# Attention and token/channel mixer on one core: q and k turned by VectorE in 32x32 blocks, scores of four heads as four 32-row TensorE tiles

## The chip, the cores and the metric

The kernel runs on one core of a Trainium2 chip. The metric is the device time of one launch in microseconds (us). Three runs of the kernel before gave 339.78, 341.17 and 840.59 us; their median is 341.17 us. The profile is one further execution of the same program.

## What is computed

Eight batches; q, k and v have 8 heads of 576 tokens and 64 features. Attention has a causal mask and a bias that comes from a running sum; behind it stand a mixer over the tokens and one over the channels, each with a residual.

```python
scores = np.matmul(q, k.transpose(0, 1, 3, 2)) / np.sqrt(D)
cum = np.cumsum(np.maximum(s, 0.0), axis=-1)
bias = -(cum[:, :, :, None] - cum[:, :, None, :])
scores = np.where(causal, -1e9, scores + np.minimum(bias, 0.0))
attn = softmax(scores)                       # over the keys
x = matmul(attn, v), heads side by side      # (8, 576, 512)
h = np.maximum(x.T @ w_tok1, 0.0) @ w_tok2   # 576 -> 256 -> 576
u = x + h.T
out = u + np.maximum(u @ w_ch1, 0.0) @ w_ch2 # 512 -> 1536 -> 512
```

## The kernel before, in words

**Layout and loops.** The program handles one batch after another, and in a batch one pair of heads after another (`pair`, L606). The bias is folded into v: v of each head is multiplied by the exponential of the running sum, with an added column of those weights, so that the division at the end gives the softmax. Of the score matrix only the diagonal 128x128 blocks and the ones beside them are computed (five key blocks, `PIECES`, L526); a flag that is worked out on the way sends inputs for which that isn't enough to `general`, which these inputs don't reach.

**The way of q and k** (the part that is changed). `stage_qk` (L563) loads k and q of two heads: 96 partitions, each with six tokens in a row of both heads (288 KB for each DMA, L568). A cast to bf16 on GpSimd (L575; in batch 0 VectorE and ScalarE may take it too) writes `qkn`. In `pair`, TensorE transposes it against the identity, six transposes of 96 columns for k and six for q (L619), into PSUM tiles of the ring `psc`. Copies then put the columns into token order in SBUF: one for k into `kT` (L629 on ScalarE or L631 on VectorE), two for q into `qT` (L639 or L641). `qT` has two planes, one for each head, whose other 64 partitions are zero, so that one matmul over 128 partitions gives one head's scores of 64 features.

**Scores.** Four PSUM tiles a pair, with five matmuls (L657): three of 512 columns, one of 384, one of 128, for both heads together. ScalarE takes the exponential (L663) into `E`, VectorE multiplies the diagonal blocks by the triangle `keep` (L671). Then nine matmuls of 65 columns a head give attention times v (L689) into the ring `pav`; VectorE takes the reciprocal (L698) and writes `x` (L703).

**Mixers.** `tok` (L773): L791 and L812 with the residual add L819, then transposes of u on TensorE (L831) with a copy (L839 or L841). `chan` (L845): L859, 48 matmuls a batch of 512 columns for even and 2x320 for odd batches, with the relu on ScalarE (L866) or VectorE (L868); L877, twelve matmuls for each output tile, the add L888 and the store. These use the ring `pmx`.

**What sets the order.** All of this is recorded as operations with planned durations (`Plan`, L47). `Plan.run` (L95) places them on the engines by readiness and priority, and the program is written out in that order; each engine then takes its instructions strictly in it. A ring (`Ring`, L15) is a set of buffers; `slot_time` (L113) says when the next one is free. PSUM has eight tiles of 512 floats: 3 `psc`, 2 `pav`, 3 `pmx`. In the first 45 planned microseconds gaps on TensorE are filled with matmuls on zeros (L964). The sum of squares of k and q (L588, and L600 with a second load for batches 0 and 1, `stage_sq`) belongs to the flag.

The rings that the change touches, as they stand:

```python
r_qf = ring("qkf", 3, [PR, 2, 2, R, D], FP32)
r_qn = ring("qkn", 3, [PR, 2, R, 2, D], BF16)
r_qT = ring("qT", 3, [128, 2, S], BF16)
r_kT = ring("kT", 3, [128, 640], BF16)
r_E = ring("E", 3, [128, 2, EW], BF16)
```

Of the kernel before, what the change touches and what calls it, by code (L numbers as in the profile page):

```python
# [46 lines left out]
class Plan:  # L47
# [47 lines left out]
    def run(self, eps=0.03):  # L95
# [17 lines left out]
        def slot_time(o):  # L113
            t = 0.0
            want = {}
            for b in o.bufs:
                if b.slot is None:
                    r = b.ring
                    if b.ordered and r.queue[0] is not b:
                        return None  # L120
                    fr = [r.free[i] for i in range(len(r.tiles)) if not r.busy[i]]
                    if not fr:
                        return None
                    t = max(t, min(fr))
                    want[id(r)] = want.get(id(r), 0) + 1
# [208 lines left out]
def kernel(  # L334
# [27 lines left out]
    R = 6  # L362
    PR = S // R

# [65 lines left out]
    def pads(eng, i):  # L430
        eng.memset(r_qT.tiles[i][64:128, 0, :], 0.0)
        eng.memset(r_qT.tiles[i][0:64, 1, :], 0.0)
        eng.memset(r_kT.tiles[i][:, S:640], 0.0)
# [8 lines left out]
    def pads3(eng, p):  # L442
        eng.memset(r_vp[p].tiles[0][64 * (1 - p) : 64 * (1 - p) + 64, NJ - 1, :, :], 0.0)
# [3 lines left out]
    for i in range(1, 3):  # L447
# [13 lines left out]
    wT = sb("wT", [128, NJ + 1, B * H], FP32, fast)  # L461
# [24 lines left out]
    def w_tr():  # L486
        for jc in range(NJ + 1):
            j0 = jc * 128 if jc < NJ else S - 128
            nc.tensor.transpose(out=bw.t[:, jc * 64 : jc * 64 + 64], in_=wn[:, j0 : j0 + 128],
                                identity=identf[:, :])  # L490
    P.op({"PE": (0.7, 1.1, w_tr)}, reads=["wn"], writes=[(bw, 0)], prio=(0,))
    P.op(dve(384, lambda: nc.vector.tensor_copy(
        out=wT[:, :, :].rearrange("p c e -> p (c e)"), in_=bw.t[:, 0:384])),
# [6 lines left out]
    NSQ = B * H // 2  # L500
    sq = sb("sq", [PR, NSQ], FP32, fast)
    junk = sb("junk", [PR, 4 * R * D], BF16, fast)
    pre = sb("pre", [64, S], FP32, fast)
# [22 lines left out]
    PIECES = [[(0, 0, 256)], [(1, 128, 384)], [(2, 256, 512)], [(3, 384, 576), (4, 512, 576)]]  # L526
# [3 lines left out]
    def stage_v(b):  # L530
        vf, vp = Buf(r_vf), Buf(r_vp[b % 2])
        odd = b % 2
        vbuf[b] = vp
        for c in range(NJ):
            n = min(128, S - c * 128)
            p0 = 64 if odd and n < 128 else 0

            def load(c=c, n=n, p0=p0):
                nc.sync.dma_start(out=vf.t[p0 : p0 + n, c, :, :],
                                  in_=v[b, :, c * 128 : c * 128 + n, :].rearrange("h p d -> p h d"))  # L540
            load_op(load, [(vf, c)] + ([("st", "v")] if b == 1 else []), 1024 * 0.0226 / 16 * n / 128)
        for c in range(NJ):
            n = min(128, S - c * 128)
            p0 = 64 if odd and n < 128 else 0

            def mul(eng, c=c, n=n, p0=p0):
                cw = c + 1 if p0 else c
                eng.tensor_tensor(  # L548
                    out=vp.t[p0 : p0 + n, c, :, 0:D], in0=vf.t[p0 : p0 + n, c, :, :],
                    in1=wT[p0 : p0 + n, cw, b * H : b * H + H].unsqueeze(2).to_broadcast([n, H, D]), op=ALU.mult)  # L550
# [4 lines left out]
        def ones():  # L555
            nc.gpsimd.tensor_copy(out=vp.t[:, 0 : NJ - 1, :, D], in_=wT[:, 0 : NJ - 1, b * H : b * H + H])
            p0, cw = (64, NJ) if odd else (0, NJ - 1)
            nc.gpsimd.tensor_copy(out=vp.t[p0 : p0 + 64, NJ - 1, :, D], in_=wT[p0 : p0 + 64, cw, b * H : b * H + H])
        P.op({"POOL": (0.5, 0.7, ones)}, reads=["wT"], writes=[(vp, "w")], prio=b * 10 + 5)

    qkn = {}

    def stage_qk(b, h):  # L563
        f, n = Buf(r_qf), Buf(r_qn)
        qkn[(b, h)] = n
        for i, src in enumerate((k, q)):
            def load(i=i, src=src):
                nc.sync.dma_start(out=f.t[:, i, :, :, :].rearrange("p e r d -> p e (r d)"),  # L568
                                  in_=src[b, h : h + 2, :, :].rearrange("e (p r) d -> p e (r d)", r=R))
# [443 lines left out]
```

## Time and profile before

| what | value |
|---|---|
| three runs | 339.78, 341.17, 840.59 us; median 341.17 |
| span of the profiled execution, first to last instruction | 337.3 us |
| its own device time | the page gives the span alone; the two lower runs lie 2.5 and 3.9 us above it |
| TensorE busy | 315.2 us (93%), granted clock 0.994 |
| ScalarE, VectorE, GpSimd busy | 221.6, 207.7, 100.1 us (66, 62, 30%) |
| DMA | 50.6 MB, 56.7% of 16 engines' time |

Read the table with two things in mind. "Busy" is a union of spans: a matmul's span runs from its first to its last column through the array, so matmuls overlap and a stream of them shows no gap; what one more matmul costs is the distance of starts, not its span. And the share is a mean over stages: in the first 50 us TensorE also runs the zero matmuls, which are there to fill gaps.

### The profile page before, as it was taken

The page shows a single profiled execution, that of the slowest core. Times are in us where ns is not written, and L with a number is a line of the kernel's source. Part 1 is how long each engine was busy: PE and PEld are TensorE (multiplying, and loading weights), DVE is VectorE, ACT ScalarE, POOL GpSimd, SP SyncE. Part 2 cuts the span into 40 slices and gives each one's busy share as a digit, 9 for nine tenths or more (in the row PEclk, how much of TensorE's full clock was granted, in tenths as well). Part 3 has the DMA queues.
Part 4 walks back from the last instruction along what each step waited for, and adds up shares of the span by engine and source line. Part 5 has one row for each costly group of instructions (what it writes and reads, how often), then busy time and mean ns, then how long its engine had stood idle before and what let it go on. Part 6 is the DMA issues. An engine that isn't in the chain of part 4 may idle for free.

```text
span 337.3 us, 6710 instructions
## 1 busy us (share of the span) xinstructions
PE 315.2 (93%) x2532; PEld 184.7 (55%) x2565; DVE 207.7 (62%) x510; ACT 221.6 (66%) x395; POOL 100.1 (30%) x137
## 2 busy tenths in 40 slices
PE   6978999988999999989999999989999999999992
PEld 2445585645765455555765445555765454446641
DVE  7698945899776746584577655584677545450021
ACT  4766975669788548785786747787799738325600
POOL 6355157768237001830147001830110000000000
PEclk9799999999999999999999999999999999999999
DMA  7999999999953349288024952253548110011031
GB/s 203 222 291 376 374 213 231 266 271 227 215 114 106 130 138 206 77 208 194 2 75 133 227 145 71 87 157 121 143 119 232 67 63 2 16 49 62 3 95 68
DMA packets 62584, 50.60 MB, mean 150 GB/s; under 512 B 39632, under 2 KB 55568, under 8 KB 62544
## 3 DMA queue, kind: packets, MB, share of 16 engines
q1 hardware_dynamic: 62544, 50.10, 56.7%
q8 instruction: 22, 0.36, 0.4%
q14 instruction: 18, 0.15, 0.2%
HBM read 40.65 MB, written 9.44 MB: 148 GB/s over the span
## 4 chain that ended last, share of the span: by engine, by line
PE 69%; DVE 18%; ACT 7%; issue 2%; DMA 1%; POOL 1%; SPq 0%; ACTq 0%
PE pmx_118 L877 9%; PE pmx_119 L877 8%; PE pmx_117 L859 8%; PE pmx_118 L859 8%; PE pmx_119 L859 8%; PE pmx_117 L877 7%; DVE ub_101 L819 3%; PE pmx_119 L791 2%; DVE E_86 L671 2%; PE psc_114 L657 2%; PE pav_115 L689 2%; PE psc_113 L657 2%; DVE E_84 L671 2%; PE pav_116 L689 2%; PE psc_112 L657 2%
## 5 line engine op out<-in xcount | busy, mean ns | idle before, releaser
L859 PEld LDWEIGHTS <-wc_70 128*128 128x128 bf16 x624 | 59.3, 98 | 30.5 <-issue 0.2
L877 PEld LDWEIGHTS <-gb_107 128*128 128x128 bf16 x240 | 22.9, 98 | 25.3
L575 POOL CAST qkn_76<-qkf_73 96x768 bf16<-96x768 f32 x22 | 19.1, 887 | 37.5 <-ACT gb_107 L866 20.1
L877 PEld LDWEIGHTS <-ga_106 128*128 128x128 bf16 x192 | 18.2, 98 | 21.2 <-issue 1.4
L575 POOL CAST qkn_77<-qkf_74 96x768 bf16<-96x768 f32 x19 | 15.7, 840 | 40.8 <-ACT ga_106 L866 19.7
L575 POOL CAST qkn_75<-qkf_72 96x768 bf16<-96x768 f32 x19 | 15.4, 828 | 39.1 <-ACT gb_107 L866 18.5
L671 DVE TENSOR_TENSOR E_84<-E_84,keep 128x256 bf16<-128x256 bf16 (+1 forms) x55 | 18.4, 365 | 13.3 <-ACT E_84 L663 12.8
L859 PE MATMUL pmx_118<-uTb_105,wc_70 128*128 128x320 bf16 x128 | 22.6, 299 | 0.1
L859 PE MATMUL pmx_117<-uTb_105,wc_70 128*128 128x320 bf16 x128 | 22.6, 299 | 0.0
L859 PE MATMUL pmx_119<-uTb_105,wc_70 128*128 128x320 bf16 x128 | 22.6, 299 | 0.0
L877 PE MATMUL pmx_119<-wc_71,gb_107 128*128 128x512 bf16 x92 | 22.3, 379 | 0.2
L548 POOL TENSOR_TENSOR vp_90<-vf_88,wT 128x512 bf16<-128x512 f32 (+1 forms) x20 | 21.0, 1069 | 2.5 <-DMA vf_88<-in_v_dram 2.2
L671 DVE TENSOR_TENSOR E_86<-E_86,keep 128x256 bf16<-128x256 bf16 (+1 forms) x50 | 17.1, 368 | 6.7 <-ACT E_86 L663 6.4
L671 DVE TENSOR_TENSOR E_85<-E_85,keep 128x256 bf16<-128x256 bf16 (+1 forms) x55 | 16.5, 329 | 6.3 <-ACT E_85 L663 6.1
L877 PE MATMUL pmx_118<-wc_71,gb_107 128*128 128x512 bf16 x80 | 19.2, 379 | 0.2
L866 ACT ACTIVATE gb_107<-pmx_119 128x320 bf16<-128x320 f32 x25 | 11.1, 444 | 11.4 <-PE pmx_119 L859 9.9
L859 PE MATMUL pmx_118<-uTa_104,wc_70 128*128 128x512 bf16 (+1 forms) x77 | 17.0, 335 | 0.2
L859 PE MATMUL pmx_119<-uTa_104,wc_70 128*128 128x512 bf16 (+1 forms) x79 | 17.1, 336 | 0.1
L548 POOL TENSOR_TENSOR vp_89<-vf_87,wT 128x512 bf16<-128x512 f32 (+1 forms) x15 | 15.3, 1040 | 5.8 <-PE pav_116 L689 4.7
L859 PE MATMUL pmx_117<-uTa_104,wc_70 128*128 128x512 bf16 (+1 forms) x78 | 16.8, 335 | 0.1
L877 PE MATMUL pmx_117<-wc_71,ga_106 128*128 128x512 bf16 x69 | 16.7, 379 | 0.2
L877 PE MATMUL pmx_118<-wc_71,ga_106 128*128 128x512 bf16 x69 | 16.5, 379 | 0.3 <-ACT uTb_105 L839 0.2
(297 smaller groups left out, 723.0 us busy)
## 6 DMA issues: line engine op xcount, KB each, us to landing
qkf_74<-in_k_dram SPq DMA_DIRECT2D x15, 288.0 KB, 3.4
qkf_74<-in_q_dram SPq DMA_DIRECT2D x15, 288.0 KB, 4.0
vf_87<-in_v_dram SPq DMA_DIRECT2D x16, 256.0 KB, 7.0
vf_88<-in_v_dram SPq DMA_DIRECT2D x16, 256.0 KB, 5.5
qkf_72<-in_k_dram SPq DMA_DIRECT2D x13, 288.0 KB, 4.0
qkf_72<-in_q_dram SPq DMA_DIRECT2D x13, 288.0 KB, 4.5
qkf_73<-in_k_dram SPq DMA_DIRECT2D x12, 288.0 KB, 4.7
qkf_73<-in_q_dram SPq DMA_DIRECT2D x12, 288.0 KB, 5.0
```

What stands on the lines that cost most here:

```text
L548: eng.tensor_tensor(out=vp.t[p0 : p0 + n, c, :, 0:D], in0=vf.t[p0 : p0 + n, c, :, :], in1=wT[p0 : p0 + n, cw, b * H : b * H + H].unsqueeze ...
L575: nc.gpsimd.tensor_copy(out=o, in_=a)
L657: nc.tensor.matmul(out=o[:, :, c0 : c0 + e - a], lhsT=kT.t[:, j0 : j0 + 128], rhs=qT.t[:, :, a:e], start=True, stop=True)
L671: nc.vector.tensor_tensor(out=E.t[:, :, d0 : d0 + n], in0=E.t[:, :, d0 : d0 + n], in1=keep[:, k0 : k0 + n].unsqueeze(1).to_broadcast([128, ...
L689: nc.tensor.matmul(out=o[:, ic, 0 : D + 1], lhsT=E.t[:, hh, d0 : d0 + 128], rhs=vp.t[:, jc, h + hh, 0 : D + 1], start=(jc == j_lo), stop=( ...
L791: nc.tensor.matmul(out=pm.t[:, ha * D : hb * D], lhsT=w1[:, NJ if odd and c == NJ - 1 else c, t * 128 : t * 128 + 128], rhs=x.t[:, c, ha * ...
L819: nc.vector.tensor_tensor(out=dst.t[lo:hi, di, :], in0=pm.t[lo:hi, :], in1=x.t[lo:hi, c, :], op=ALU.add)
L859: nc.tensor.matmul(out=pm.t[:, 0 : e - a], lhsT=wc1[:, m, cc * 128 : cc * 128 + 128], rhs=uT.t[:, m, a:e], start=(m == 0), stop=(m == NMC ...
L866: lambda cc=cc, pm=pm, a=a, e=e: nc.scalar.activation(out=g.t[:, cc, a:e], in_=pm.t[:, 0 : e - a], func=AF.Relu),
L877: nc.tensor.matmul(out=pm.t[:, :], lhsT=g.t[:, cc, c * 128 : c * 128 + 128], rhs=wc2[:, cc, :], start=(cc == 0), stop=(cc == NCC - 1))
```

## The change

The counts of heads and buffers change, and with them the way of k and q:

- A load takes one of k or q for four heads: partition 32e+t holds 18 tokens in a row of head e (`[128, 1152]`, 4608 bytes in a row, 576 KB a DMA). Four such buffers.
- VectorE transposes that buffer in 32x32 blocks, in fp32, one instruction for each load (L574 of the changed kernel, STREAM_TRANSPOSE). The features of head e then lie on partitions 32e to 32e+31, in two halves of 32 features.
- GpSimd casts each half to bf16 and puts it in token order (L582; two for k, two for q of four heads; in batch 0 VectorE and ScalarE may take them). TensorE's transposes L619 and the copies L629, L631, L639, L641 are gone, and so are the zeros in `qT`.
- Scores of four heads are computed in two phases. In each, a key block takes two matmuls a head (one for each half of the features, added up in PSUM), each over 32 partitions, with `tile_position` at row 32e and a PSUM tile of its own for each head. That is 40 matmuls for four heads.
- The exponential is taken for one head at a time, 512 columns as before; the mask multiply covers four heads at once.
- PSUM: 4 `psc`, which one phase fills, and 4 `pmx`, which now also take attention times v. `kT`, `qT` and `E` have two buffers, each for four heads.
- The squares read the fp32 load, one instruction for k and one for q of four heads.
- v's last rows lie on the same partitions for even and odd batches. `slot_time` now counts how many buffers of a ring an operation wants. A branch that would transpose u by DMA is added for batches from 9 on (`UDMA = 9`); there are eight, so it is never taken.

Its core as a diff:

```diff
-                    fr = [r.free[i] for i in range(len(r.tiles)) if not r.busy[i]]
-                    if not fr:
+                    fr = sorted(r.free[i] for i in range(len(r.tiles)) if not r.busy[i])
+                    n = want[id(r)] = want.get(id(r), 0) + 1
+                    if len(fr) < n:
                         return None
-                    t = max(t, min(fr))
-                    want[id(r)] = want.get(id(r), 0) + 1
+                    t = max(t, fr[n - 1])
...
-    R = 6
-    PR = S // R
+    UDMA = 9
+    HQ = 4
+    TP = 128 // HQ
+    R = S // TP
+    DQ = D // 32
...
-    r_qf = ring("qkf", 3, [PR, 2, 2, R, D], FP32)
-    r_qn = ring("qkn", 3, [PR, 2, R, 2, D], BF16)
-    r_qT = ring("qT", 3, [128, 2, S], BF16)
-    r_kT = ring("kT", 3, [128, 640], BF16)
-    r_E = ring("E", 3, [128, 2, EW], BF16)
+    r_qf = ring("qkf", 4, [128, R * D], FP32)
+    r_t1 = ring("qkt", 3, [128, R, DQ, TP], FP32)
+    r_qT = ring("qT", 2, [128, DQ, S], BF16)
+    r_kT = ring("kT", 2, [128, DQ, 640], BF16)
+    r_E = ring("E", 2, [128, HQ, EW], BF16)
...
-    r_sc = ring("psc", 3, [128, 512], FP32, psum)
-    r_av = ring("pav", 2, [128, 512], FP32, psum)
-    r_mx = ring("pmx", 3, [128, 512], FP32, psum)
+    r_sc = ring("psc", 4, [128, 512], FP32, psum)
+    r_mx = ring("pmx", 4, [128, 512], FP32, psum)
...
-    PIECES = [[(0, 0, 256)], [(1, 128, 384)], [(2, 256, 512)], [(3, 384, 576), (4, 512, 576)]]
+    PHASES = [[(0, 0, 256), (1, 128, 384)], [(2, 256, 512), (3, 384, 576), (4, 512, 576)]]
...
+    def load_qk(f, b, h, i):
+        def load():
+            nc.sync.dma_start(out=f.t[:, :], in_=SRC[i][b, h : h + HQ, :, :].rearrange("e (t r) d -> (e t) (r d)", r=R))
+        load_op(load, [(f, 0)], 1.65)
...
     def stage_qk(b, h):
+        for i in range(2):
+            f, t1, T = Buf(r_qf), Buf(r_t1), Buf((r_kT, r_qT)[i])
+            qkt[(b, h, i)] = T
+            load_qk(f, b, h, i)
+            P.op(dve(R * D, lambda f=f, t1=t1: nc.vector.transpose(
+                out=t1.t[:, :, :, :].rearrange("p r q t -> p (r q t)"), in_=f.t[:, :])),
+                reads=[(f, 0)], writes=[(t1, 0)], holds=[T], prio=2 if b else -1)
+            for qq in range(DQ):
+                def cast(e, qq=qq, t1=t1, T=T):
+                    o = T.t[:, qq, 0:S].rearrange("p (t r) -> p t r", r=R)
+                    a = t1.t[:, :, qq, :].rearrange("p r t -> p t r")
+                    if e == 0:
+                        nc.gpsimd.tensor_copy(out=o, in_=a)
...
+                alts = {"POOL": (*c_pool(S, 0.0017), lambda cast=cast: cast(0))}
...
-            P.op({"PE": (R * 0.045, R * 0.045 + 0.3, tr)}, reads=[(nat, ti)] + pads, writes=[(pt, 0)], holds=[dst], prio=(np_, 2))
...
+        for ph, blocks in enumerate(PHASES):
+            ps = [Buf(r_sc, False) for e in range(HQ)]
...
             def mm(ps=ps, cols=cols):
-                o = ps.t[:, :].rearrange("p (e n) -> p e n", e=2)
-                for (jc, a, e, c0) in cols:
-                    j0 = S - 128 if odd and jc == NJ - 1 else jc * 128
-                    nc.tensor.matmul(out=o[:, :, c0 : c0 + e - a], lhsT=kT.t[:, j0 : j0 + 128],
-                                     rhs=qT.t[:, :, a:e], start=True, stop=True)
+                for (jc, a, z, c0) in cols:
+                    for qq in range(DQ):
+                        for e in range(HQ):
+                            p0 = e * TP
+                            nc.tensor.matmul(out=ps[e].t[:, c0 : c0 + z - a],
+                                             lhsT=kT.t[p0 : p0 + TP, qq, jc * 128 : jc * 128 + 128],
+                                             rhs=qT.t[p0 : p0 + TP, qq, a:z], start=(qq == 0), stop=(qq == DQ - 1),
+                                             tile_position=(p0, 0))
...
+            for e in range(HQ):
+                def ex(p=ps[e], e=e, ph=ph):
+                    nc.scalar.activation(out=E.t[:, e, ph * 512 : ph * 512 + 512], in_=p.t[:, :], func=AF.Exp, scale=0.125)
...
-                        in1=keep[:, k0 : k0 + n].unsqueeze(1).to_broadcast([128, 2, n]), op=ALU.mult)
+                        in1=keep[:, 0:n].unsqueeze(1).to_broadcast([128, HQ, n]), op=ALU.mult)
...
-        for hh in range(2):
-            pa, rc = Buf(r_av, False), Buf(r_rc, False)
+        for hh in range(HQ):
+            pa, rc = Buf(r_mx, False), Buf(r_rc, False)
```

**TensorE, the way from k to the scores.** Before, k and q of a pair pass through TensorE and then give five score matmuls. The first two rows are one of the six transposes of a tensor (`qkn` is the bf16 cast, `psc` the PSUM tile), the others, from further on in the program, the last four score matmuls of a pair with their weight loads (`kT` is the stationary side, `qT` the moving one):

```order
L619 LDWEIGHTS qkn1_76
L619 MATMUL psc2_114<-ident_64,qkn1_76 128x96
...
L657 MATMUL psc1_113<-qT2_80,kT2_83 128x512
...
L657 MATMUL psc2_114<-qT2_80,kT2_83 128x512
...
L657 MATMUL psc0_112<-qT2_80,kT2_83 128x2x192
L657 LDWEIGHTS kT2_83
L657 MATMUL psc0_112<-qT2_80,kT2_83 128x2x64
```

In the changed kernel the same place reads as follows, right behind the token mixer's matmuls (L779):

```order
L779 MATMUL pmx0_114<-h11_97,w2_69 128x512
L622 LDWEIGHTS kT0_81
L622 MATMUL psc0_110<-qT0_79,kT0_81 128x256
L622 LDWEIGHTS kT0_81
L622 MATMUL psc1_111<-qT0_79,kT0_81 128x256
L622 LDWEIGHTS kT0_81
L622 MATMUL psc2_112<-qT0_79,kT0_81 128x256
L622 LDWEIGHTS kT0_81
L622 MATMUL psc3_113<-qT0_79,kT0_81 128x256
```

The transposes have gone from TensorE. A group of four matmuls, one for each head, writes the four PSUM tiles in turn, and each matmul has a weight load of its own.

**VectorE, between two score phases.** Before, the copies of `qT` stand among masks (`E`), relus of the channel mixer (`ga`) and reciprocals:

```order
L641 COPY qT_78<-psc_112 64x576 [waits PE_49]
L671 TENSOR_TENSOR E_84<-E_84,keep 128x2x128 [waits Activation_49]
L868 TENSOR_SCALAR ga_106<-pmx_118 128x512 [waits PE_49]
L671 TENSOR_TENSOR E_84<-E_84,keep 128x2x128 [waits Activation_49] x2
L868 TENSOR_SCALAR ga_106<-pmx_117 128x512 [waits PE_49]
```

In the changed kernel a comparable stretch (`qkf` is the load, `qkt` the transposed buffer, `gb` the channel mixer's relu) reads:

```order
L840 TENSOR_SCALAR gb_105<-pmx_115 128x320 [waits PE_49]
L574 STREAM_TRANSPOSE qkt_76<-qkf_75 128x1152 [waits DMAHW3_49,Pool_49]
L840 TENSOR_SCALAR gb_105<-pmx_114 128x320 [waits PE_49]
L840 TENSOR_SCALAR gb_105<-pmx_117 128x320 [waits PE_49]
L638 TENSOR_TENSOR E_83<-E_83,keep 128x4x128 [waits Activation_49]
L638 TENSOR_TENSOR E_83<-E_83,keep 128x4x128
L574 STREAM_TRANSPOSE qkt_77<-qkf_72 128x1152 [waits DMAHW5_49,Pool_49]
L840 TENSOR_SCALAR gb_105<-pmx_114 128x320 [waits PE_49]
```

The copies out of PSUM are replaced by transposes that wait for a load and for GpSimd (which must have emptied a `qkt` buffer), and the relus that free TensorE's PSUM tiles stand right behind them.

More of the change, by code (lines that the diff above doesn't have):

```diff
@@ L535, in stage_v, with load @@
             n = min(128, S - c * 128)
-            p0 = 64 if odd and n < 128 else 0
-            def load(c=c, n=n, p0=p0):
-                nc.sync.dma_start(out=vf.t[p0 : p0 + n, c, :, :],
+            def load(c=c, n=n):
+                nc.sync.dma_start(out=vf.t[0:n, c, :, :],
                                   in_=v[b, :, c * 128 : c * 128 + n, :].rearrange("h p d -> p h d"))
@@ L604, with quad @@
+    def stage_sq(b, h):
+        for i in range(2):
+            f = Buf(r_qf)
+            load_qk(f, b, h, i)
+            square(f, b, h, i)
     xbuf = {}
-    def pair(b, h):
+    def quad(b, h):
         np_ = (b * H + h) / 2
-        nat = qkn[(b, h)]
-        npair = (b * H + h) // 2
-        pads = [("pad", npair)] if 0 < npair < 3 else []
-        qT, kT, E = Buf(r_qT), Buf(r_kT), Buf(r_E)
+        nq = (b * H + h) // HQ
+        pads = [("pad", nq)] if 0 < nq < 2 else []
+        kT, qT, E = qkt[(b, h, 0)], qkt[(b, h, 1)], Buf(r_E)
```

178 lines of the change are left out of this document (61 added, 117 removed).

## The prediction

> **What bounds the kernel now.** I read first the busy times, then the chain of work that ended last, then the busy time by stretches.
>
> ```profile
> PE 315.2 (93%) x2532; PEld 184.7 (55%) x2565; DVE 207.7 (62%) x510; ACT 221.6 (66%) x395; POOL 100.1 (30%) x137
> PE 69%; DVE 18%; ACT 7%; issue 2%; DMA 1%; POOL 1%; SPq 0%; ACTq 0%
> 0.00:50.00 50.00, 43.43 (x368) 27.19 (x374) 38.99 (x101) 34.20 (x59) 23.17 (x44) 0.97 1.04 281
> 50.00:331.30 281.30, 271.74 (x2166) 157.55 (x2191) 168.10 (x409) 187.45 (x337) 76.89 (x94) 1.00 0.50 129
> ```
>
> The last two rows are stretches of time: length, then busy time and count of TensorE, its weight loads, VectorE, ScalarE and GpSimd, then the granted clock and the DMA share. From 50 us to the last matmul TensorE is busy for 271.7 of 281.3 us at full clock, so only 9.6 us are left in which it waits. No other engine passes 67% there. TensorE is the bound, and what an instruction costs is the distance at which the next one starts:
>
> ```profile
> 183.23 0.42 PE L619 MATMUL psc_113<-ident,qkn_75 96*128 96x96 bf16 x6
> 183.48 0.42 PE L619 MATMUL psc_114<-ident,qkn_76 96*128 96x96 bf16 x6
> 183.74 0.39 PE L831 MATMUL pmx_119<-ident,ua_100 128*128 128x128 bf16 x4
> ...
> 194.78 0.43 PE L689 MATMUL pav_115<-vp_90,E_84 128*128 128x65 bf16 x9
> 195.05 0.43 PE L689 MATMUL pav_116<-vp_90,E_84 128*128 128x65 bf16 x9
> ...
> 198.78 0.38 PE L657 MATMUL psc_114<-qT_79,kT_82 128*128 128x512 bf16 x1
> 198.99 0.38 PE L657 MATMUL psc_112<-qT_79,kT_82 128*128 128x512 bf16 x1
> 199.21 0.38 PE L657 MATMUL psc_113<-qT_79,kT_82 128*128 128x512 bf16 x1
> ```
>
> Start and span of merged pieces. Six transposes take 0.255 us (183.23 to 183.74 for twelve). A score matmul of 512 columns takes 0.215 us, though its span is 0.38: its result ends 0.165 us after the next has started. Nine narrow matmuls, each with a weight load, take 0.27 us: a pair of load and matmul cannot follow faster than 0.030 us here.
>
> **What leaves TensorE.** The first 41 us contain gap fillers, so work that leaves there only makes room for more zeros. Rows of transposes and of scores from 50 us on (between 41.3 us and 50 us there are none of either):
>
> ```profile
> 50.00:337.30 287.30, 18.54 (x312) 16.07 (x312) 1.00 0.49 127
> 50.00:337.30 287.30, 32.60 (x130) 12.51 (x130) 1.00 0.49 127
> ```
>
> The first row is L619, the second L657; columns are TensorE and its loads. 312/6 = 52 groups of transposes by 0.255 us are 13.3 us. 130/5 = 26 pairs by four PSUM tiles of 512 columns by 0.215 us are 22.4 us. In all 35.7 us.
>
> **What comes back.** In the changed order two and a half sets of four heads stand ahead of the first channel matmul, so 13.5 sets remain. A set has 40 matmuls with 8192 columns. No row shows two matmuls that run at once, so I bound a set: all four heads side by side cost 2048 columns, 4 x 0.215 = 0.86 us; one after another 16 x 0.215 = 3.44 us; at the pace of the narrow matmuls 40 x 0.030 = 1.20 us. I take 1.20: the four matmuls of a group read other partitions and write other PSUM tiles, nothing in the program orders them, and each has a weight load, as the narrow ones have. Each of the two phases also changes from matmuls over 128 rows to 32-row tiles and back. The nearest row is the 0.165 us by which a result outlasts the next start: 0 to 0.165 for each of four changes, and I take half, 0.33 us a set. A set then costs 1.53 us, 13.5 sets 20.7 us; the ends are 11.6 (0.86, no change cost) and 55.4 us (3.44 + 0.66). TensorE is relieved by 35.7 - 20.7 = 15.0 us.
>
> The Trainium skill, TensorEngine Tiling, Key Properties, says that changing the tiling mode drains TensorE. By it every change costs the full 0.165 us, a set 1.86 us, the relief is 10.6 us instead of 15.0 and the time 332 us; with no such cost it is 19.5 us and 323. No run here shows it yet. The same skill, in TensorE: Matmul & The Clock Gate, table of Part 3 under "Measured speedup vs the span model", gives 3.07 times for four row tiles of 512 columns; that speaks against the rival of matmuls one after another.
>
> **The other engines**, which must stay under TensorE's time. Rows: L629, L639, L631, L641, L671, L575 over the whole span, then single operations:
>
> ```profile
> sum 337.30, ACT 14.71; mean ACT 7.36
> sum 337.30, ACT 23.41; mean ACT 11.71
> sum 337.30, DVE 6.77; mean DVE 3.39
> sum 337.30, DVE 20.30; mean DVE 10.15
> sum 337.30, DVE 51.99; mean DVE 26.00
> sum 337.30, POOL 49.94; mean POOL 24.97
> 4.23 0.39 DVE L473 TENSOR_SCALAR s_sb<-s_sb 64x576 f32<-64x576 f32 x1
> 4.65 1.35 DVE L475 TENSOR_TENSOR_SCAN cum<-one_sb,s_sb 64x576 f32<-64x576 f32 x1
> L888 DVE TENSOR_TENSOR of_109<-pmx_118,ua_100 128x512 f32<-128x512 f32 x4 | 2.8, 692 | 8.5 <-PE pmx_118 L877 8.5
> L703 DVE TENSOR_TENSOR x_91<-pav_115,rc_94 128x320 bf16<-128x320 f32 x6 | 2.9, 488 | 0.2
> L698 DVE RECIPROCAL rc_94<-pav_115 128x5 f32<-128x5 f32 x16 | 3.0, 188 | 5.4 <-PE pav_115 L689 5.4
> L671 DVE TENSOR_TENSOR E_85<-E_85,keep x55: 209/282/1318, 15.7 to 287.2; 128x256 bf16<-128x256 bf16 x44, 128x128 bf16<-128x128 bf16 x11
> ```
>
> Four copy lines fall away: 38.1 us of ScalarE, 27.1 us of VectorE. In their place stand 32 block transposes of 1152 fp32 elements. By the fp32 rows an element takes from 0.68 ns (L473) to 2.34 ns (the scan), so 0.78 to 2.7 us each; I take one element a step, the slope between L888 and L703 (204 ns for 192 elements, 1.06 ns) with their fixed 0.15 us: 1.37 us, 44 us in all (25 to 86). Masks: their row (L671) gives least, middle and longest; from 0.21 us for 128 elements to 0.28 for 256, four heads of 128 come to about 0.42, and 64 x 0.42 + 16 x 0.28 = 31 us instead of 52. VectorE ends at 207.7 - 27.1 + 44 - 21 = 204 us (up to 246), under TensorE's some 300.
>
> ```profile
> L588 ACT ACTIVATE junk<-qkn_77 96x1536 bf16<-96x1536 bf16 x8 | 11.9, 1489 | 0.1
> L575 POOL CAST qkn_76<-qkf_73 96x768 bf16<-96x768 f32 x22 | 19.1, 887 | 37.5 <-ACT gb_107 L866 20.1
> L548 POOL TENSOR_TENSOR vp_90<-vf_88,wT 128x512 bf16<-128x512 f32 (+1 forms) x20 | 21.0, 1069 | 2.5 <-DMA vf_88<-in_v_dram 2.2
> ```
>
> The 32 squares shrink from 1536 to 1152 elements, 1.49 to 1.12 us; with the copies ScalarE falls to about 172 us. GpSimd's order shows 59 half casts of 576 elements that step through the source: at the cast's 1.15 ns an element 0.66 us, at the two-input multiply's 2.09 ns 1.20 us. I take 1.20, the upper row, since the stepping has no row: 71 us instead of 50, GpSimd about 121 us, hidden with more than half its time free. If a cast took 2.0 us, GpSimd would hold 168 us and still not be the bound.
>
> **Queues.** A block transpose waits in VectorE's order for a load and for a `qkt` buffer that GpSimd frees; the relus behind it free TensorE's PSUM tiles. Alone its 1.37 us is covered: the three other `pmx` tiles hold three channel groups of four matmuls, 3 x 0.54 = 1.6 us even at 320 columns (320/512 of 0.215 us each). Behind a four-head attention block, which needs all four `pmx` tiles and 4 x (0.19 + 0.49) us of VectorE, cover is gone. Bounds: nothing, to 14 sets x 1.37 = 19 us. I take 2.5 us, a quarter of today's 9.6 us of waits, because such meetings are few. The longest mask, 1.32 us against 0.28, shows VectorE being held up by something else already; with half as many masks that should not grow.
>
> **The start.** The channel mixer begins when batch 0 has passed attention and its weights have landed:
>
> ```profile
> GB/s 203 222 291 376 374 213 231 266 271 227 215 114 106 130 138 206 77 208 194 2 75 133 227 145 71 87 157 121 143 119 232 67 63 2 16 49 62 3 95 68
> qkf_74<-in_k_dram SPq DMA_DIRECT2D x15, 288.0 KB, 3.4
> 41.27 0.60 PE L859 MATMUL pmx_117<-uTa_104,wc_70 128*128 128x256 bf16 x4
> ```
>
> A slice is 8.4 us. Twelve k and q loads of 288 KB (3.5 MB), for one and a half batches, lie ahead of or among the weights; at 203 GB/s, the first slice, they take 17 us, at 376, where the weights run, 9.4. Rows three times as long may come nearer to the latter: a gain of up to 4 us if half of it shows. Against it, the first score waits for four heads instead of two (288 KB more of k at 203 GB/s, 1.5 us) and for a transpose of 1.37 us: a loss of up to 2.8. I take a gain of 1.5 us.
>
> **Sum.** Span 337.3 - 15.0 - 1.5 + 2.5 = 323.3 us, a change of -14.0. The median of the runs, 341.2, lies 3.9 us above the span; the change goes to it: **327 us**.
>
> **Rivals.**
> - *More.* Side by side at full rate with cheap changes: 35.7 - 11.6 = 24.1 us off, with the start's 4: 313 us. For it: nothing forbids it; against it: 40 weight loads a set at the pace of the narrow rows.
> - *Eaten by waits.* VectorE's queue, held by GpSimd and by PSUM tiles taken four at a time, gives back some 12 us instead of 2.5: 337 us, no measurable change. For it: VectorE holds 18% of the present chain, and the new chain from load over VectorE and GpSimd to TensorE runs through two queues. Against it: every engine but TensorE has a third of its time free.
> - *Slower.* The 32-row matmuls run one after another: a set costs 3.44 + 0.33 = 3.77 us, 13.5 sets 50.9 us, 15.2 more than leaves: 341.2 + 15.2 - 1.5 + 2.5 = 357 us. It decides from (35.7 - 1.0)/13.5 = 2.57 us a set, an overlap of only about 1.5. For it: no row shows overlap. Against it: separate rows, partitions and PSUM tiles.
> - *It doesn't do what it says:* if the second half of the features had to wait until the first had landed in the same PSUM tile, a group would cost a whole span. L859's piece above holds four 256-column matmuls, starts 0.11 apart, in 0.60 us, so a span is 0.27 us; ten groups and the changes make 3.0 us a set, 40.5 us for all, 347 us. I count it with the waits.
>
> **Chances.** Forecast 0.56, more 0.12, eaten by waits 0.17, slower 0.15. A measurement of this kernel tells some 2% (7 us) from no change: faster (under 334) 0.68, same 0.17, slower 0.15. The forecast's own range is 320 to 334. For 8 in 10 I take 314 to 345 us: down to the case of more, up through the waits, and only the serial case is left out.
>
> **What would show it.** Right: no L619; 40 score matmuls of a set (L622) between 1.2 and 1.9 us from first start of a phase to the next line's start, summed over both phases; starts within a group closer than 0.05 us; VectorE near 204, GpSimd near 121, ScalarE near 172 us; the first channel matmul near 40 us; TensorE's waits after 50 us near 12 us. Wrong: score groups whose starts lie a full 0.11 us apart for each head, block transposes over 2 us, or TensorE waiting over 20 us for VectorE's relus.

## The result, and the profile after

The changed kernel takes **331.89 us** (median of 4 runs, 328.70 to 332.10), the kernel before 340.48 (median of its three runs and a fourth, 338.58); the ratio is 0.974 (95% interval 0.968 to 0.979). Faster, by 8.6 us. The profiled execution took 332.1 us, its span is 330.2. The rows of the page that answer to the first ones of the prediction, then the stretches before and after 50 us, the latter up to the last matmul:

```profile
PE 301.5 (91%) x2658; PEld 170.8 (52%) x2658; DVE 224.7 (68%) x433; ACT 173.2 (52%) x328; POOL 121.1 (37%) x129
...
PE 52%; DVE 25%; SPq 8%; DMA 6%; issue 6%; ACT 1%; DVEq 0%; ACTq 0%
```

```profile
0.00:50.00 50.00, 44.69 (x415) 27.21 (x416) 40.19 (x86) 30.47 (x54) 23.93 (x36) 0.93 0.99 319
50.00:324.20 274.20, 256.78 (x2245) 143.54 (x2242) 183.86 (x347) 142.77 (x274) 97.16 (x94) 0.98 0.45 125
```

TensorE lost work, but it now waits for 17.4 of 274.2 us instead of 9.6 of 281.3, and its clock is no longer full. In the chain that ended last it fell from 69 to 52%, VectorE rose from 18 to 25%.

**Where TensorE's gain is.** Two phases of one set of scores, between channel matmuls; start and span of merged pieces:

```profile
157.73 0.43 PE L831 MATMUL pmx<-uTb,wc 128*128 128x320 bf16 x2
...
158.10 0.61 PE L622 MATMUL psc<-qT,kT 32*128 32x256 bf16 x16
...
158.65 0.45 PE L831 MATMUL pmx<-uTb,wc 128*128 128x320 bf16 x2
```

```profile
161.10 0.43 PE L831 MATMUL pmx<-uTb,wc 128*128 128x320 bf16 x2
161.47 0.62 PE L622 MATMUL psc<-qT,kT 32*128 32x256 bf16 x24
162.02 0.45 PE L831 MATMUL pmx<-uTb,wc 128*128 128x320 bf16 x2
```

A phase lasts 0.55 us from its first start to the next line's start. A channel matmul of 320 columns has the next 0.134 us behind it (320/512 of 0.215), so the phase at 158.10 could have started at 157.73 + 0.27 = 158.00 and that at 161.47 at 161.37: another 0.10 us goes on entering. A set thus costs 2 x 0.65 = 1.30 us. From the first channel matmul to the last matmul stand 544 score matmuls, 13.6 sets, 17.7 us; 35.7 us left. The relief is 18.0 us.

**Where it went.** That stretch, from the first channel matmul to the last matmul, before and after (columns as above):

```profile
41.27:331.30 290.03, 280.47 (x2246) 165.37 (x2271) 172.36 (x418) 194.49 (x351) 81.22 (x98) 1.00 0.52 132
36.11:324.20 288.09, 270.55 (x2377) 154.50 (x2374) 193.66 (x364) 153.62 (x300) 104.66 (x100) 0.98 0.47 134
```

It became 1.9 us shorter instead of 18.0. Of the 16.1 us that are missing, 8.0 are waits (17.5 instead of 9.6). The other 8.1 appear in the distances of starts, with the clock as the nearest cause: its record has 13.7 us at half speed between 50 us and the last matmul (before: none), worth 6.8 us at most. In sum the span is 337.3 - 5.2 (the start, 36.11 instead of 41.27) - 18.0 + 16.1 = 330.2 us. The waits:

```profile
PE pmx L656 <- DVE E L638: 8.7, 10, 2.1
PE pmx L656 <- DVE x L670: 3.7, 2, 3.4
PE pmx L656 <- DVE of L860: 2.3, 3, 1.3
```

The three largest, 14.7 us in 15 waits over the whole span, are attention times v (L656) behind VectorE: the masks (L638), the normalization that frees its PSUM tile (L670), an output add. The longest in the order of time, VectorE, GpSimd and L656:

```profile
57.34 2.30 POOL L582 CAST kT<-qkt 128x576 bf16<-128x576 f32 x2 [2.07 <-PE pmx L656]
...
59.07 0.43 PE L656 MATMUL pmx<-vp,E 128*128 128x65 bf16 x9 [1.30 <-DVE of L860]
...
59.11 3.25 DVE L638 TENSOR_TENSOR E<-E,keep 128x512 bf16<-128x512 bf16 x3
59.59 2.63 POOL L582 CAST qT<-qkt 128x576 bf16<-128x576 f32 x2
62.18 2.08 POOL L543 TENSOR_TENSOR vp<-vf,wT 128x512 bf16<-128x512 f32 x2
62.29 0.18 DVE L665 RECIPROCAL rc<-pmx 128x5 f32<-128x5 f32 x1
62.39 0.84 DVE L670 TENSOR_TENSOR x<-pmx,rc 128x320 bf16<-128x320 f32 x2
62.89 0.82 PE L656 MATMUL pmx<-vp,E 128*128 128x65 bf16 x12 [3.39 <-DVE x L670]
```

Three masks take 3.25 us, 1.08 each, while GpSimd casts. The reciprocal and the normalization stand behind them in VectorE's order, and TensorE waits 3.39 us for those. The masks' spread (least, median, longest), their total and two neighbours on VectorE:

```profile
L638 DVE TENSOR_TENSOR E<-E,keep x80: 272/421/1659, 14.1 to 273.3; 128x512 bf16<-128x512 bf16 x64, 128x256 bf16<-128x256 bf16 x16
```

```profile
L638 DVE TENSOR_TENSOR E<-E,keep 128x512 bf16<-128x512 bf16 (+1 forms) x80 | 54.0, 723 | 1.7 <-ACT E L631 1.7
...
L574 DVE STREAM_TRANSPOSE qkt<-qkf 128x1152 f32<-128x1152 f32 x32 | 43.5, 1363 | 0.6 <-DMA qkf<-in_q_dram 0.5
...
L670 DVE TENSOR_TENSOR x<-pmx,rc 128x320 bf16<-128x320 f32 x64 | 29.1, 483 | 0.8
```

The median is the 0.42 us that the prediction used, but the mean is 0.72: 54.0 us instead of 31, 23 of them lost to something that holds masks up. The plan counts such a mask at 0.34 us.

### The profile page after: what moved, and what is told of

The parts are those of the page before. It is cut to its first block, busy times and chain, and to the rows that moved or that the text cites. A ratio compares the mean times of both kernels' runs of the same rounds, so it can differ in the third digit from the quotient of the medians.

```text
span 330.2 us, 6745 instructions
## 1 busy us (share of the span) xinstructions
PE 301.5 (91%) x2658; PEld 170.8 (52%) x2658; DVE 224.7 (68%) x433; ACT 173.2 (52%) x328; POOL 121.1 (37%) x129
## 4 chain that ended last, share of the span: by engine, by line
PE 52%; DVE 25%; SPq 8%; DMA 6%; issue 6%; ACT 1%; DVEq 0%; ACTq 0%
PE pmx L849 21%; PE pmx L831 18%; DVE E L638 8%; SPq L536 7%; PE pmx L758 6%; DVE qkt L574 4%; PE pmx L656 4%; DVE ub L786 3%; DMA qkf<-in_q_dram 2%; DVE ua L786 2%; DMA uTb<-in_moe_w_tok_dram 2%; PE psc L622 2%; DMA qkf<-in_k_dram 2%; DVE of L860 1%; DVE gb L840 1%
## 5 line engine op out<-in xcount | busy, mean ns | idle before, releaser
L631 ACT ACTIVATE E<-psc 128x512 bf16<-128x512 f32 x128 | 66.0, 603 | 40.8 <-PE psc L622 40.4
L831 PEld LDWEIGHTS <-wc 128*128 128x128 bf16 x624 | 60.5, 99 | 36.0 <-issue 3.5
L582 POOL CAST kT<-qkt 128x576 bf16<-128x576 f32 x31 | 37.2, 1231 | 95.5 <-DVE qkt L574 84.5
L831 PE MATMUL pmx<-uTb,wc 128*128 128x320 bf16 x384 | 56.0, 304 | 1.8 <-DVE gb L840 1.0
L638 DVE TENSOR_TENSOR E<-E,keep 128x512 bf16<-128x512 bf16 (+1 forms) x80 | 54.0, 723 | 1.7 <-ACT E L631 1.7
L565 ACT ACTIVATE junk<-qkf 128x1152 bf16<-128x1152 f32 x32 | 37.4, 1168 | 33.5 <-DMA qkf<-in_k_dram 21.0
L849 PE MATMUL pmx<-wc,gb 128*128 128x512 bf16 x240 | 53.4, 379 | 0.0
L849 PE MATMUL pmx<-wc,ga 128*128 128x512 bf16 x192 | 45.0, 384 | 0.0
L574 DVE STREAM_TRANSPOSE qkt<-qkf 128x1152 f32<-128x1152 f32 x32 | 43.5, 1363 | 0.6 <-DMA qkf<-in_q_dram 0.5
L831 PE MATMUL pmx<-uTa,wc 128*128 128x512 bf16 (+1 forms) x240 | 43.5, 337 | 0.2 <-DVE x L670 0.2
L656 PE MATMUL pmx<-vp,E 128*128 128x65 bf16 x576 | 27.4, 202 | 15.3 <-DVE E L638 8.7
L543 POOL TENSOR_TENSOR vp<-vf,wT 128x512 bf16<-128x512 f32 (+1 forms) x35 | 36.8, 1086 | 5.8 <-PE pmx L656 5.8
L582 POOL CAST qT<-qkt 128x576 bf16<-128x576 f32 x28 | 34.2, 1250 | 8.7 <-DVE qkt L574 8.6
L656 PEld LDWEIGHTS <-E 128*128 128x128 bf16 x576 | 23.6, 103 | 23.0 <-DVE E L638 10.1
L670 DVE TENSOR_TENSOR x<-pmx,rc 128x320 bf16<-128x320 f32 x64 | 29.1, 483 | 0.8
L622 PE MATMUL psc<-qT,kT 32*128 32x256 bf16 (+2 forms) x640 | 20.5, 252 | 0.6 <-ACT qT L586 0.5
```

The source lines that it names most:

```text
L543: eng.tensor_tensor(out=vp.t[0:n, c, :, 0:D], in0=vf.t[0:n, c, :, :], in1=wT[0:n, c, b * H : b * H + H].unsqueeze(2).to_broadcast([n, H, D ...
L565: P.op({"ACT": (1.1, 1.5, lambda: nc.scalar.activation(out=junk[:, :], in_=f.t[:, :], func=AF.Square, accum_out=sq[:, col : col + 1]))}, r ...
L574: P.op(dve(R * D, lambda f=f, t1=t1: nc.vector.transpose(out=t1.t[:, :, :, :].rearrange("p r q t -> p (r q t)"), in_=f.t[:, :])), reads=[( ...
L582: nc.gpsimd.tensor_copy(out=o, in_=a)
L622: nc.tensor.matmul(out=ps[e].t[:, c0 : c0 + z - a], lhsT=kT.t[p0 : p0 + TP, qq, jc * 128 : jc * 128 + 128], rhs=qT.t[p0 : p0 + TP, qq, a:z ...
L631: nc.scalar.activation(out=E.t[:, e, ph * 512 : ph * 512 + 512], in_=p.t[:, :], func=AF.Exp, scale=0.125)
```

## Experiments

Theory A: VectorE's in-order queue is overfull around the attention blocks, chiefly because GpSimd's casts hold up the masks; attention times v pays. Rivals: the queue is full of block transposes whatever the masks do; the shared PSUM tiles; the half clock by itself. Except for the edit shown or named, each kernel is the changed one.

**Casts almost without work**

```diff
+                    if b > 0:
+                        o, a = o[:, 0:1, :], a[:, 0:1, :]
                     if e == 0:
                         nc.gpsimd.tensor_copy(out=o, in_=a)
```

> The changed kernel with the same instructions in the same order, but from batch 1 on each half cast on GpSimd moves 18 of its 576 elements, so the scores of those batches are computed from the first batch's columns. Theory: GpSimd's casts (1.19 us each) hold up VectorE's mask multiplies, which read two SBUF operands (80 of them take 54.0 us, 0.72 mean, against 0.42 for the middle one); attention times v waits for the masks and TensorE then falls to half clock. Then the masks fall to 0.5 us mean or less, TensorE's waits after 50 us from 17 to under 10 us, no half clock stands behind the first channel matmul, and the time is 317 to 323 us. Rival 1, the block transposes in VectorE's queue: masks stay over 0.65, time 329 to 333. Rival 2, the 32-row matmuls themselves pull the clock down: half clock between 60 and 95 us stays.

319.37 us, ratio 0.936 (0.927 to 0.946). In the same order the masks need 18 us less:

```profile
L640 DVE TENSOR_TENSOR E<-E,keep 128x512 bf16<-128x512 bf16 (+1 forms) x80 | 36.0, 497 | 2.5 <-ACT E L633 2.5
```

GpSimd's casts do lengthen the masks, and taking them away is worth 12.5 us. The waits for masks fall from 8.7 to 3.2 us. The longest wait stays, and with it 6.8 us at half clock, where none were expected: in that place GpSimd now multiplies v (L543), and three masks are as long beside that as beside casts.

```profile
57.80 5.45 POOL L543 TENSOR_TENSOR vp<-vf,wT 128x512 bf16<-128x512 f32 x5
...
58.08 3.27 DVE L640 TENSOR_TENSOR E<-E,keep 128x512 bf16<-128x512 bf16 x3
...
61.88 0.82 PE L658 MATMUL pmx<-vp,E 128*128 128x65 bf16 x12 [3.41 <-DVE x L672]
```

So it is GpSimd's work, casts or not, that goes with long masks. In the changed kernel TensorE waited for casts for only 0.5 us (at L622, in batch 0), so that is not how they cost.

**Block transposes almost without work**

```diff
-            P.op(dve(R * D, lambda f=f, t1=t1: nc.vector.transpose(
-                out=t1.t[:, :, :, :].rearrange("p r q t -> p (r q t)"), in_=f.t[:, :])),
+            n = R if b == 0 else 1
+            P.op(dve(R * D, lambda f=f, t1=t1, n=n: nc.vector.transpose(
+                out=t1.t[:, 0:n, :, :].rearrange("p r q t -> p (r q t)"), in_=f.t[:, 0 : n * D])),
```

> The changed kernel with the same instructions in the same order, but from batch 1 on each block transpose on VectorE handles 64 of its 1152 elements, so later batches use left-over columns. VectorE loses some 28 transposes by 1.2 us, 33 us of work, while GpSimd keeps all its casts. Theory of the casts holding up the masks: the masks still take 0.65 us or more, the time falls by little, 326 to 331 us. Rival, the transposes in VectorE's queue are what attention times v waits for: 316 to 323 us.

320.77 us, ratio 0.940 (0.932 to 0.948): the rival's number. The masks are as long as before, yet nearly the same time comes back:

```profile
L639 DVE TENSOR_TENSOR E<-E,keep 128x512 bf16<-128x512 bf16 (+1 forms) x80 | 52.5, 703 | 2.7 <-ACT E L632 2.7
```

So the long masks are not the whole cause. Each relief of VectorE by itself returns 11 to 12.5 of the 16.1 us, which points to its queue. The run also speaks on the half clock: its record has 13.7 us at half speed, as in the changed kernel, and yet the stretch from the first channel matmul on is 11.4 us shorter, 9.3 of them waits.

```profile
36.25:312.90 276.65, 268.43 (x2377) 153.72 (x2374) 165.60 (x363) 153.51 (x300) 104.19 (x100) 0.98 0.48 139
```

The half clock by itself is therefore not what cost these 11 us.

**Both at once**: the short block transposes, and the casts on ScalarE as in the next run.

> Leaves out part of the computation: from the second batch on the block transposes move 64 of 1152 columns; and the casts of those batches go to ScalarE, as in the run with the casts there (320.4 us), whose order of work it keeps. If the casts on GpSimd and the transposes on VectorE each lengthen one and the same queue (VectorE's), of which only the overload costs time, the second relief finds little left: 315 to 319 us. If each had a cost of its own on the path (11 to 12 us each when taken alone), they add up: 308 to 311 us.

315.64 us, ratio 0.929 (0.923 to 0.935). The second relief brings some 5 us more, and both together return 16.2 us, all of the 16.1 that were missing. That fits one queue of which only the overload costs. It does not prove it: no more than 16.1 us were missing, and to add up to 22.6 us (11.1 and 11.5) the reliefs would also have had to take nearly all of the 6.7 us of waits that this run has left from the first channel matmul on.

**Casts of the later batches on ScalarE**, nothing left out:

```diff
                 if b == 0:
                     alts["DVE"] = (*c_dve(S), lambda cast=cast: cast(1))
                     alts["ACT"] = (*c_act(S), lambda cast=cast: cast(2))
+                else:
+                    alts = {"ACT": (1.2, 1.45, lambda cast=cast: cast(2))}
```

> The changed kernel with the casts of batches 1 to 7 on ScalarE instead of GpSimd (1.20 us each by the three casts of batch 0 there); nothing is left out. Theory of the casts holding up the masks: masks 0.5 us mean or less, 319 to 326 us although ScalarE rises from 173 to about 235 us. Rival, VectorE's queue is long by itself: no gain, 329 to 336 us, since ScalarE's exponentials and relus now also stand behind casts.

320.38 us, ratio 0.939 (0.931 to 0.947). The whole work is done, and the 11.5 us stay: a cast takes 1.20 us on ScalarE, and the masks are short with it there. VectorE's busy time is 223.1 us all the same, hardly under the 224.7 of the changed kernel, since the plan gives it relus that ScalarE had; so its total is not the measure, but what stands in its order ahead of attention times v.

```profile
L640 DVE TENSOR_TENSOR E<-E,keep 128x512 bf16<-128x512 bf16 (+1 forms) x80 | 35.4, 490 | 2.4 <-ACT E L633 2.3
...
L586 ACT CAST qT<-qkt 128x576 bf16<-128x576 f32 x30 | 35.0, 1198 | 3.4 <-DVE qkt L574 3.3
```

**The plan told the mask's real price**

```diff
-                P.op(dve(HQ * n, mk, True), reads=[(E, ph, e) for e in range(HQ)], writes=[(E, "m", jc)], prio=0)
+                P.op({"DVE": (0.78 * n / 128, 0.78 * n / 128 + 0.22, mk)}, reads=[(E, ph, e) for e in range(HQ)], writes=[(E, "m", jc)], prio=0)
```

> The changed kernel, nothing left out, with one number of the plan changed: a triangular mask of 128x512 is given to the planner at 0.78 us (its mean in the changed kernel's trace is 0.72 over both shapes) instead of 0.34. The order of the work and the share of the relus between VectorE and ScalarE follow from that. Theory A (VectorE's in-order queue is overfull because the plan believes that it has room, and attention x v waits behind it): relus move to ScalarE, VectorE falls from 225 to about 205 us, the waits of attention x v for masks and outputs halve, 320 to 326 us. Theory B (each single mask, lengthened by a GpSimd cast beside it, lies on the path from the exponential to attention x v, whatever else VectorE does): the waits stay, 329 to 333 us.

324.50 us, ratio 0.953 (0.950 to 0.956). Masks are almost as long as in the changed kernel, but the waits for them fall from 8.7 to 1.8 us:

```profile
L638 DVE TENSOR_TENSOR E<-E,keep 128x512 bf16<-128x512 bf16 (+1 forms) x80 | 50.3, 676 | 6.8 <-ACT E L631 6.6
```

```profile
PE pmx L656 <- DVE x L670: 3.6, 2, 2.9
PE pmx L656 <- DVE E L638: 1.8, 3, 1.2
```

The plan moved relus to ScalarE (188 us busy over the stretches up to 320 us, 173 before) and left less on VectorE (210 instead of 223). One number of the plan is worth 7.4 us.

**Both remedies**: the casts on ScalarE, and a mask of 128x512 priced at its mean there, 0.49 us.

> The kernel with the casts of the later batches on ScalarE, nothing left out, and a mask of 128x512 given to the planner at 0.49 us, its mean there, instead of 0.34. If VectorE's queue, as planned, is still what attention x v waits for in 50 to 100 us: 316 to 319 us. If what is left is fixed by the data (transfers of q and k, the chain within a batch): 319 to 322 us.

317.55 us, ratio 0.934 (0.929 to 0.939). From the first channel matmul on:

```profile
37.84:309.10 271.26, 264.23 (x2350) 151.42 (x2349) 188.79 (x384) 192.84 (x320) 41.79 (x47) 0.99 0.48 139
```

Here 520 score matmuls, 13 sets, stand in it, so the relief is 35.7 - 13 x 1.30 = 18.8 us, and 290.0 - 18.8 = 271.2. The stretch lasts 271.3 us: as long as the old one less the whole relief of TensorE. That is no floor, since the same stretch of the next run, with 520 score matmuls too, lasts 267.9 us (it begins 2.0 us later).

**All prices**: the casts on ScalarE, a mask of 128x512 priced at 0.58 us, and VectorE and ScalarE with measured fixed costs.

```diff
-    occ = 0.07 + n * 0.000833 + (0.093 if bias else 0.0)
+    occ = 0.18 + n * 0.000833 + (0.093 if bias else 0.0)
...
-    occ = 0.07 + n * (0.00053 if two else 0.00104)
+    occ = 0.16 + n * (0.00053 if two else 0.00104)
```

> The kernel with the casts of the later batches on ScalarE, nothing left out, with every fixed cost that the plan uses set to what the trace shows: VectorE 0.16 us an instruction instead of 0.07 (a block transpose then counts 1.36 us, an add of 512 0.69), ScalarE 0.18 instead of 0.07 (an exponential 0.61), a mask of 128x512 0.58. If a plan with true prices takes the last waits of attention x v away: 314 to 317 us. If the run with the mask's price alone (317.6 us) already had all of it, since its span from the first channel matmul on is already the old one less the relief of TensorE: 316 to 319 us.

317.08 us, ratio 0.933 (0.925 to 0.941): no different from the run before. The mask's price and the place of the casts had all of it. Of the versions that leave nothing out these two are the best, 14 to 15 us under the changed kernel.

**Part of the casts back on GpSimd**, under the same prices but for a cast on GpSimd, which the plan now counts at 1.25 us (the diff is against the run with all prices):

```diff
-                alts = {"POOL": (*c_pool(S, 0.0017), lambda cast=cast: cast(0))}
+                alts = {"POOL": (*c_pool(S, 0.0020), lambda cast=cast: cast(0))}
...
-                    alts = {"ACT": (1.2, 1.45, lambda cast=cast: cast(2))}
+                    alts["ACT"] = (1.2, 1.45, lambda cast=cast: cast(2))
```

> As the run with all prices, but a cast of the later batches may go to ScalarE (1.20 us) or to GpSimd (1.25 us), as the plan chooses; it leaves about half on GpSimd. If collisions of GpSimd with the masks cost time whenever VectorE is near full, masks get longer than 0.53 us in the mean and the time is 318 to 323 us. If the plan with true prices has enough room on VectorE to absorb them: 315 to 318 us, as without them.

328.19 us, ratio 0.962 (0.953 to 0.971), worse than the range of either. 37 casts on GpSimd (4 in the run before) are enough to bring the long masks back:

```profile
L640 DVE TENSOR_TENSOR E<-E,keep 128x512 bf16<-128x512 bf16 (+1 forms) x80 | 49.6, 668 | 4.2 <-ACT E L633 4.1
```

The first channel matmul also came late, at 44.9 us instead of 39.9: of the 14.5 us between the two spans (328.2 and 313.7), 5.1 lie in the start, for a reason that was not looked into. The run therefore does not price the masks alone.

**A PSUM tile for attention times v**

```diff
-    r_mx = ring("pmx", 4, [128, 512], FP32, psum)
+    r_mx = ring("pmx", 3, [128, 512], FP32, psum)
+    r_av = ring("pav", 1, [128, 512], FP32, psum)
```

> The changed kernel, nothing left out, with one of its four shared pmx tiles given to attention x v alone (pmx 3, pav 1), in the direction of the kernel before, which had pav 2 and pmx 3. The order of the work follows from the plan with these tiles. Theory A (VectorE's overfull queue, not the sharing of PSUM tiles, is what attention x v waits for): no gain, 330 to 337 us, with attention x v still waiting for masks and normalizations. Rival (attention x v now competes with the channel matmuls for PSUM tiles, and lost its own): 322 to 328 us.

341.00 us, ratio 1.003 (0.999 to 1.006). The gain that the rival expected did not come, and my own range was missed too: with one tile each head waits for the normalization of the head before it. What the sharing of tiles costs by itself is therefore not settled by this run.

```profile
PE pav L657 <- DVE x L671: 8.3, 7, 2.1
PE pav L657 <- DVE E L639: 3.3, 4, 1.0
```

Four shared tiles are better than three and one. Two and three, as before, would leave three for the scores, of which a phase needs four; it was not tried.

**More dummy matmuls**: `WARM = 100.0` instead of 45.

> The changed kernel, nothing left out, with the dummy matmuls that fill planned gaps of TensorE kept up until 100 us of the plan instead of 45: 21 dummy matmuls more (about 4.5 us), all else in the same order. Theory A (the three stretches at half clock after 60 us follow from TensorE standing idle, and cost some 5 us of the 16.9 that were lost): fewer of them in the record of the clock, 326 to 330 us. Theory B (the half clock has a cause of its own, or the dummies stand at the wrong places, since the plan's gaps are not the real ones): as many stretches at half clock, 331 to 336 us.

330.97 us, ratio 0.973 (0.970 to 0.976), between the two ranges and no different from the changed kernel. The clock did change:

```profile
50.00:75.00 25.00, 22.70 (x258) 11.86 (x255) 20.49 (x37) 15.89 (x30) 21.65 (x22) 1.00 1.01 259
75.00:100.00 25.00, 19.51 (x224) 12.86 (x225) 23.77 (x44) 17.35 (x35) 15.93 (x17) 0.93 0.56 157
```

It is 1.00 and 0.93 where the changed kernel has 0.86 and 0.86, so dummies in the gaps keep it up; but these dummies are themselves 4.8 us of TensorE's busy time, and attention still waits (9.1 us for masks). More clock alone did not make the kernel faster. What the half clock costs by itself stays open, since the dummies may have eaten the gain.

**Scores head by head**

```diff
-                for (jc, a, z, c0) in cols:
-                    for qq in range(DQ):
-                        for e in range(HQ):
+                for e in range(HQ):
+                    for (jc, a, z, c0) in cols:
+                        for qq in range(DQ):
```

> The changed kernel with the score matmuls of a phase ordered head by head, so that neighbours in TensorE's queue use the same 32 rows; nothing is left out. Theory: the gain on TensorE comes from four row tiles that run at once and needs neighbours on different rows. Then a phase takes 1.7 us or more instead of 0.55, a set of four heads some 2.3 us more, and the time is 352 to 362 us. Rival, the 32-row matmuls are short each by themselves, or the order does not matter: 330 to 334 us.

338.16 us, ratio 0.993 (0.989 to 0.998). Slower by 6 us, between the two ranges and far from one matmul after another; the 16 matmuls of a first phase keep their 0.57 us, the 24 of a second take 1.25:

```profile
162.49 0.65 PE L622 MATMUL psc<-qT,kT 32*128 32x256 bf16 x16
163.06 0.31 PE L831 MATMUL pmx<-uTb,wc 128*128 128x320 bf16 x1
```

```profile
165.89 1.32 PE L622 MATMUL psc<-qT,kT 32*128 32x256 bf16 x24
167.14 0.45 PE L831 MATMUL pmx<-uTb,wc 128*128 128x320 bf16 x2
```

The overlap of the row tiles is real and rests partly on the order in which they are issued.

## Why the prediction was right, and where it was wrong

The kernel became faster, and by the mechanism that was forecast; the time came 5 us above the forecast and within its own range (320 to 334). Two terms were better than said, by 3.0 and 3.7 us, and one was worse by 13.6. That the errors half cancelled, and that the time still lies in the range, is in part luck.

- **Relief of TensorE**: -15.0 forecast, -18.0 measured. The choice of 0.030 us a matmul, the pace of the narrow ones, was wrong: the tiles run side by side at full rate, 0.86 us a set, plus 0.44 us around its two phases (1.30 - 0.86). That is 0.11 for each of four changes; I took 0.08 of at most 0.165. The starts within a group lie 3 ns apart, under the 0.05 us asked for. By the sign as it was written, from the first start of a phase to the next line's start, a set takes 1.10 us and lies under the 1.2 to 1.9 that were named. The Trainium skill (TensorEngine Tiling, Key Properties) says that changing the tiling mode drains TensorE. Priced at 0.165 us, as the prediction did, four drains would cost 0.66 us; the 0.44 measured are two thirds of that.
- **Start**: -1.5 forecast, -5.2 measured (36.11 instead of near 40). The loads did come nearer to the rate of long rows: 244 to 400 GB/s in the first five slices of the page instead of 203 to 376; packets under 2 KB fell from 55,568 to 39,568. That this made the gain was not tested; with the same loads the first channel matmul came between 34.9 and 44.9 us in the other runs, so the loads are not all that sets it.
- **Waits**: +2.5 forecast, 16.1 lost. This is the step that failed. Of the 16.1 only 8.0 are longer waits; the other 8.1 stand in the distances of starts, for which the sum has no term, since it reckons with the full clock of the kernel before. The bounds, 0 to 19 us, held the total; the choice inside them did not. "Such meetings are few" is wrong: every attention block puts masks, reciprocals and normalizations of four heads into VectorE's one order.
- **Masks**: "with half as many masks that should not grow" is the sentence that failed beneath it. I took 31 us; they took 54.0, although there were 80 instead of 160. At the 0.28 and 0.21 us of the prediction 128 and 32 masks before come to 43 us, so some 9 us of 52 were holdup; now it is 23 in 54. GpSimd works 121 us instead of 100, and each mask is twice as large; which of the two counts for more was not tested. VectorE hence 224.7 instead of 204; without these 23 us it would be at 202.
- **Right**: block transposes 1.363 us (1.37), casts 1.23 and 1.25 (1.20), ScalarE 173.2 (172), GpSimd 121.1 (121). TensorE's waits after 50 us, 17.4 us, are more than the 12 expected; but those for VectorE's relus, of which 20 us were to refute the forecast, are only some 1.3 us (L840): a block transpose ahead of the relus was the wrong place to look.
- **The rivals.** "Eaten by waits" had the mechanism, 12 us given back by VectorE's queue held by GpSimd, and was given 0.17; its size was exceeded, and only the larger relief and the better start kept the kernel faster. The holdup was in sight: the row of L671 before, 282 ns in the median and 1318 at most, was read and then not carried over to a larger load on GpSimd.

The Trainium skill had the rule: SBUF — State Buffer, "Who interferes with whom", says that a VectorE instruction with two inputs in SBUF contends with a GpSimd instruction that reads SBUF, and that one with at most one SBUF input, outside the 2-port modes, does not. The trace agrees: masks read `E` and `keep` and take 0.47 us in the mean with all prices, 0.72 in the changed kernel; block transposes, with one SBUF input, take 1.363 us in the changed kernel and 1.364 with all prices, where the later casts are on ScalarE. That it is this port was not tested by itself.

What stays open is the share of the half clock in the 8.1 us outside the waits, and the 1.3 us of them that even its full price leaves. Among the runs with the same 544 score matmuls in the stretch, TensorE's busy time above the old one less the relief is 8.1 and 6.0 us where 13.7 us are at half clock (the changed kernel, short transposes), 3.9 where 6.8 are (short casts), 3.0 and 2.2 where 3.4 are (casts on ScalarE, both reliefs). That fits the clock, but the waits fall along with it, and the two were not parted.

## What to carry to other kernels

Work moved off the bounding engine counts only as far as the engines that now feed it keep their order short: look at what stands in the in-order queue between a result and the instruction that frees its tile. A two-input VectorE operation beside a busy GpSimd should be priced at its mean, not at its median, and a planner must be told that price; here the price alone was worth 7 us and the place of the casts 11. When two reliefs of one engine return nearly the same time each and not the sum together, look first whether more was there to return; here both returned all that was missing, and the cheapest full-work version (the casts elsewhere, and a true price in the plan) came within 2 us of them.

## What the hardware showed that was not expected

- Four 32-row matmuls of 256 columns start 3 ns apart and the next four 0.11 us later, the column time of one: four row tiles work at once.
- TensorE starts matmuls of other row tiles ahead of their turn. Issued head by head, four a head, the four heads' first starts lie 13 to 14 ns apart, while a head's second matmul starts 0.12 us after its first. With six a head they lie 0.24 us apart (99.63, 99.87, 100.10, 100.34 us from the span's start), and the second head's first matmul (256 columns, 99.87) still starts ahead of the first head's fourth (192 columns, 99.94). That would fit a view of only a few matmuls ahead, which was not tested.
- In the changed kernel the clock record goes to half speed in pieces of 3.4 or 6.8 us. One, from 60.7 to 67.5 us, lies around the wait of 3.39 us that ends at 62.9; the two others, from 77.6 and 91.4 us, begin inside waits of 0.85 and 0.69 us, and waits as long later on (0.95 us, ending at 151.1) have none. Of 13.7 us in 50 to 100 us, 3.4 were left with dummies of 4.8 us in the gaps.
